# The first product of a gated layer in seven block products for eight, with its weights read from DRAM

## The chip, the cores and the metric

The kernel runs on one core of one Trainium2 chip. The metric is the device time of one launch in microseconds; host work on the arguments (reshaping and reordering) is not in it. A core has TensorE (PE) for matrix products, VectorE (DVE), ScalarE (ACT) and GpSimd (POOL) for elementwise work, and SyncE (SP), whose queue issues all of this kernel's DMAs. SBUF is the on-chip memory of 128 partitions, PSUM the accumulators: eight banks of 128x512 float32, all in use here.

## The reference

```python
x = attention(q, k, v, mem_k, mem_v)     # 4 batches, 8 heads, 768 tokens, 64 dims: chunks of 32
                                         # queries against 8 + 16 + 32 + 8 keys
x = x.transpose(0, 2, 1, 3).reshape(3072, 512)
gate = 1.0 / (1.0 + np.exp(-(x @ w_gate)))        # 512 x 1536
x = (gate * (x @ w_val)) @ w_out                  # 512 x 1536, 1536 x 512
h = x @ w_in                                      # 512 x 2048
g = h * (1.0 / (1.0 + np.exp(-h)))
out = g @ w_out2                                  # 2048 x 512
```

The five weights arrive as float64; q, k and v as float32.

## The kernel before

Every number that enters a large product is kept as two float32r parts, hi + lo (`split`: ScalarE copies hi, another engine subtracts it to get lo), and every product is three matmuls: hi·hi, hi·lo, lo·hi. One matmul has a 128x128 weight and 512 columns. The feature dimension of 512 is four tiles of 128 (`KT`), so `proj` issues 4 × 3 = 12 matmuls for a tile of 128 output features and 512 tokens, and `mm3` 12 for the four tiles of an output product.

The float64 weights are loaded raw (512 KB each of 128x512) and go through a pipeline of three steps (`Unit`, `Feed`): ScalarE scales the high words (L101), VectorE joins high and low words to a float32 in three instructions (`join`, L106, L109, L113), ScalarE and GpSimd split it (`part`).

*Layer 1* runs over six blocks of 512 tokens. Each has twelve f of 128 hidden features, and for each f TensorE does a gate product `pg`, a value product `pv` and, lagging one f, the output product into four banks `y` (L486 on): 36 matmuls. ScalarE takes the sigmoid, VectorE multiplies (`gated`, L264) and g is split. The attention of block b + 1 runs beside block b (`run_events`). The first block also prepares its own weights (`feed1`). `wo` is kept as plain float32 and split anew for each f of each block by ScalarE and GpSimd (`split_wo`). The finished block is copied out of PSUM (L429) and stored to DRAM (`yd`).

*Layer 2* runs over six blocks of 512 tokens with sixteen f each: twelve matmuls `ph` (L250), sigmoid (L260), multiplication (L264), split (L76, L79), and, lagging two f, twelve matmuls into the four banks `o` (`emit_out2`). All weights of layer 2 stay in SBUF; they are prepared by `feed2` in the last block of layer 1 and the first of layer 2, in slots that come free there. The x of the next block comes back from DRAM (`y32in`) and is split at the end of the block before.

The instructions stand in the order in which the code is written (`manual_schedule`); each engine runs its own queue in order, and a tile whose ring or pool is full waits for the last user of the old one.

Of the kernel before, what the change touches and what calls it, by code (L numbers as in the profile page):

```python
# [8 lines left out]
F32 = mybir.dt.float32  # L9
# [16 lines left out]
TPB = S // P  # attention tiles per batch row  # L26
# [4 lines left out]
BLOCKS2 = [512] * 6  # L31
# [7 lines left out]
NW = 2 * NF1  # resident gate and value units  # L39
# [3 lines left out]
def moe_kernel(ctx: ExitStack, tc: tile.TileContext, qh, kh, vh, wg, wv, wo, w2i, w2o, out):  # L43
# [14 lines left out]
    def w_slot(name):  # L58
        return main.tile([P, 2, 512], F32R, tag="w", name=name, bufs=NW)

    def t_slot(name):
        return main.tile([P, 512], F32, tag="t", name=name, bufs=2)
# [28 lines left out]
    class Unit:  # L91
        def __init__(self, src, name, raw_slot=None, slot=None):
            self.src, self.name, self.raw_slot, self.slot = src, name, raw_slot, slot

        def load(self):
            self.stg = main.tile([P, 512, 2], I32, tag="stg", name=f"stg_{self.name}", bufs=4)
            nc.sync.dma_start(out=self.stg.rearrange("p a b -> p (a b)"), in_=self.src)
# [5 lines left out]
        def join(self):  # L103
            self.t = (self.raw_slot or t_slot)(f"t_{self.name}")
# [9 lines left out]
                out=self.t.bitcast(I32), in0=high, scalar=3, in1=low,  # L114
# [3 lines left out]
        def part(self):  # L118
            if self.slot is not None:
                self.u = self.slot(self.name)  # L120
                split(self.u[:, 0], self.u[:, 1], self.t, nc.gpsimd)
# [113 lines left out]
    def split_x(src, n, name, on_pool=0, hi_dve=()):  # L235
        xs = []
        for kt in range(KT):
            x = main.tile([P, 2, 512], F32R, tag="x", name=f"{name}_{kt}", bufs=5)
# [6 lines left out]
    def proj(o, w, x, n, order=((0, 0), (0, 1), (1, 0)), late=None):  # L245
        """order: the products of parts (of w, of x) of each tile; late: the one kept for the end"""
# [23 lines left out]
    with tc.manual_schedule():  # L270
        att_cm = tc.tile_pool(name="att", bufs=1, side="right")
        att = att_cm.__enter__()
        wop_cm = tc.tile_pool(name="wop", bufs=1)
        wop = wop_cm.__enter__()

        NB1, NB2 = len(BLOCKS1), len(BLOCKS2)
        n0 = BLOCKS1[0] // P

        # buffers of the running attention, and those of the first tiles in weight slots
# [54 lines left out]
        # the first tiles, a step apart; idle products beforehand wake the tensor engine's clock  # L334
# [46 lines left out]
        # attention of block b + 1 runs beside the products of block b  # L381
# [26 lines left out]
        g_t, wo_u, yacc = {}, {}, {}  # L408

        def emit_out1(bi, f):  # L410
# [3 lines left out]
            g, w = g_t.pop((bi, f)), wo_u.pop((bi, f))  # L414
# [7 lines left out]
            mm3(groups)  # L422
            if f == NF1 - 1:
# [9 lines left out]
        def load_y(bi):  # L433
            t = x32_tile(f"y32in{bi}")
            lo, hi = sum(BLOCKS2[:bi]), sum(BLOCKS2[: bi + 1])
            for j, s in enumerate(starts1):
                a, b = max(lo, s), min(hi, s + BLOCKS1[j])
                if a < b:
                    nc.sync.dma_start(out=t[:, :, a - lo : b - lo], in_=y_dram[j][:, :, a - s : b - s])
            return t  # L440

        def split_wo(bi, f):
            w = wop.tile([P, 2, 512], F32R, tag="wor", name=f"wor{bi}_{f}", bufs=1)
# [191 lines left out]
```

## Time and profile before

| | before |
|---|---|
| median of three runs | 1255.85 us (1255.69 to 1255.92) |
| span of the profiled execution | 1254.8 us |
| TensorE busy, matmuls | 1213.5 us (97%), 6655 |
| VectorE, ScalarE, GpSimd busy | 564.1, 437.1, 206.5 us |
| moved by DMA | 93.30 MB, 74 GB/s over the span |
| last block of layer 1 begins, first `ph` of layer 2's fourth f | 602.20, 736.60 us |

The page's busy shares say which engine is full; the windows say in which stage. The chain of waits, followed back from the last instruction, is TensorE for most of its length. `PEclk` is the clock that TensorE was granted, 1.00 for 2.4 GHz.

### The profile page before, as it was taken

The numbers are of one execution on the slowest core, as the hardware profiler recorded it, in microseconds if no ns is written. First come the engines' busy times: TensorE is split into PE (matmuls) and PEld (weight loads), VectorE is DVE, ScalarE is ACT, GpSimd is POOL, SyncE is SP. The second block draws the span as 40 slices with busy tenths as digits, with TensorE's granted clock in tenths as the row PEclk, the third lists the DMA queues.
The fourth block names the chain that finished last, engine by engine and source line by source line (L and its number), as shares of the span: only waits on it lengthen the run. The fifth ranks groups of instructions, "written<-read, shape, count | busy, mean of one in ns | idle before, by whom it ended". The sixth has DMA issues, their size and how long they took to land.

```text
span 1254.8 us, 15980 instructions
## 1 busy us (share of the span) xinstructions
PE 1213.5 (97%) x6655; PEld 986.8 (79%) x6655; DVE 564.1 (45%) x780; ACT 437.1 (35%) x695; POOL 206.5 (16%) x156
## 2 busy tenths in 40 slices
PE   7888999999999999999978899999999999999999
PEld 6666788888888888888756688888888888888887
DVE  7999943333324333332688862332322322323322
ACT  3555543334334333333444442222322322222222
POOL 2555521111111111111345420000000000000000
PEclk9899999999999999999999999999999999999999
DMA  9666521213112121312454320000100100100000
GB/s 309 189 194 194 158 82 61 66 54 105 53 51 84 54 70 54 109 53 85 134 147 122 118 84 1 34 34 1 68 1 1 67 1 1 68 1 1 34 1 34
DMA packets 29016, 93.30 MB, mean 74 GB/s; under 512 B 3600, under 2 KB 3856, under 8 KB 28176
## 3 DMA queue, kind: packets, MB, share of 16 engines
q1 hardware_dynamic: 28944, 92.29, 23.5%
q8 instruction: 52, 0.85, 0.3%
q14 instruction: 20, 0.16, 0.0%
HBM read 79.69 MB, written 12.58 MB: 74 GB/s over the span
## 4 chain that ended last, share of the span: by engine, by line
PE 79%; DVE 17%; DMA 2%; issue 1%; ACT 1%; SPq 0%; DVEq 0%; ACTq 0%
PE ph L250 21%; PE pv L250 11%; PE pg L250 11%; PE o L88 7%; PE o L84 7%; PE o L86 7%; PE y L84 4%; PE y L86 4%; PE y L88 4%; PE sc L179 1%; DVE stg_w2i L109 1%; PE px L219 1%; DVE t_w2o L113 1%; DVE t_wg L113 1%; DVE t_wo L113 1%; DVE stg_w2i L106 1%
## 5 line engine op out<-in xcount | busy, mean ns | idle before, releaser
L250 PE MATMUL ph<-yy,w2i 128*128 128x512 f32 x1152 | 280.8, 393 | 2.5 <-ACT yy L76 1.4
L250 PEld LDWEIGHTS ph<-yy,w2i 128*128 128x128 f32 x1152 | 216.5, 189 | 49.6 <-ACT yy L76 1.8
L250 PE MATMUL pv<-x,wv 128*128 128x512 f32 x864 | 220.6, 406 | 24.4 <-DVE sg L264 22.9
L250 PEld LDWEIGHTS pv<-x,wv 128*128 128x128 f32 x864 | 164.5, 194 | 67.6 <-DVE sg L264 17.4
L250 PE MATMUL pg<-x,wg 128*128 128x512 f32 x864 | 210.4, 392 | 2.4 <-ACT wg L76 1.0
L264 DVE TENSOR_TENSOR sgh<-ph,sgh 128x512 f32<-128x512 f32 x96 | 66.4, 692 | 286.2 <-ACT sgh L260 286.1
L250 PEld LDWEIGHTS pg<-x,wg 128*128 128x128 f32 x864 | 160.6, 188 | 38.7 <-ACT wg L76 1.8
L79 POOL TENSOR_TENSOR wor<-t_wo,wor 128x512 fp32r<-128x512 f32 x72 | 100.4, 1395 | 394.1 <-ACT wor L76 394.1
L260 ACT ACTIVATE sgh<-ph 128x512 f32<-128x512 f32 x96 | 57.5, 599 | 296.6 <-PE ph L250 294.4
L88 PE MATMUL o<-w2o,gh 128*128 128x512 f32 (+1 forms) x384 | 148.1, 386 | 0.0
L86 PE MATMUL o<-w2o,gh 128*128 128x512 f32 (+1 forms) x384 | 148.0, 385 | 0.0
L84 PE MATMUL o<-w2o,gh 128*128 128x512 f32 (+1 forms) x384 | 147.9, 385 | 0.0
L264 DVE TENSOR_TENSOR sg<-pv,sg 128x512 f32<-128x512 f32 x72 | 49.3, 684 | 114.9 <-PE pv L250 114.8
L76 ACT CAST g<-sg 128x512 fp32r<-128x512 f32 x72 | 44.7, 621 | 151.0 <-DVE sg L264 151.0
L79 DVE TENSOR_TENSOR gh<-sgh,gh 128x512 fp32r<-128x512 f32 x96 | 66.5, 693 | 65.9 <-ACT gh L76 65.9
L76 ACT CAST gh<-sgh 128x512 fp32r<-128x512 f32 x96 | 59.5, 620 | 80.1 <-DVE sgh L264 80.1
L84 PEld LDWEIGHTS o<-w2o,gh 128*128 128x128 f32 x384 | 72.1, 188 | 15.3
L86 PEld LDWEIGHTS o<-w2o,gh 128*128 128x128 f32 x384 | 72.1, 188 | 15.3
L88 PEld LDWEIGHTS o<-w2o,gh 128*128 128x128 f32 x384 | 72.1, 188 | 14.7
L84 PE MATMUL y<-g,wor 128*128 128x512 f32 x288 | 79.5, 398 | 0.6 <-ACT wor L76 0.6
L86 PE MATMUL y<-g,wor 128*128 128x512 f32 x288 | 77.2, 390 | 0.0
L88 PE MATMUL y<-g,wor 128*128 128x512 f32 x288 | 77.0, 389 | 0.0
(85 smaller groups left out, 1123.1 us busy)
## 6 DMA issues: line engine op xcount, KB each, us to landing
k<-in_kh_dram SPq DMA_DIRECT2D x24, 512.0 KB, 5.2
qA<-in_qh_dram SPq DMA_DIRECT2D x21, 512.0 KB, 3.9
vA<-in_vh_dram SPq DMA_DIRECT2D x42, 256.0 KB, 4.2
stg_w2i<-in_w2i_dram SPq DMA_DIRECT2D x16, 512.0 KB, 3.6
stg_w2o<-in_w2o_dram SPq DMA_DIRECT2D x16, 512.0 KB, 3.6
stg_wg<-in_wg_dram SPq DMA_DIRECT2D x12, 512.0 KB, 4.0
stg_wv<-in_wv_dram SPq DMA_DIRECT2D x12, 512.0 KB, 3.6
stg_wo<-in_wo_dram SPq DMA_DIRECT2D x12, 512.0 KB, 3.7
```

Source lines behind the costliest of these rows:

```text
L76: nc.scalar.copy(hi, src)
L79: lo_eng.tensor_tensor(out=lo, in0=src, in1=hi.bitcast(F32), op=ALU.subtract)
L84: nc.tensor.matmul(o, w_hi, x_hi, start=first, stop=False)
L86: nc.tensor.matmul(o, w_hi, x_lo, start=False, stop=False)
L88: nc.tensor.matmul(o, w_lo, x_hi, start=False, stop=last)
L106: nc.vector.tensor_scalar(out=low, in0=low, scalar1=29, scalar2=None, op0=ALU.logical_shift_right)
L109: nc.vector.scalar_tensor_tensor(out=low, in0=high, scalar=-2147483648, in1=low, op0=ALU.bitwise_and, op1=ALU.bitwise_or,)
L113: nc.vector.scalar_tensor_tensor(out=self.t.bitcast(I32), in0=high, scalar=3, in1=low, op0=ALU.logical_shift_left, op1=ALU.bitwise_or,)
L179: nc.tensor.matmul(scv[cp * 64 : cp * 64 + 64, c2, a], qb[:, 4 * a + c].rearrange("p u q -> p (u q)"), kt[:, a, c], start=True, stop=True,)
L250: nc.tensor.matmul(o[:, :n], w[:, pw, kt * P : (kt + 1) * P], x[kt][:, px, :n], start=i == 0, stop=i == len(steps) - 1,)
L260: nc.scalar.activation(out=sg[:, :n], in_=psg[:, :n], func=AF.Sigmoid)
L264: nc.vector.tensor_tensor(out=sg[:, :n], in0=psv[:, :n], in1=sg[:, :n], op=ALU.mult)
```

## The change

Layer 2's first product works on three blocks of 1024 tokens, two halves of 512, and on pairs of f. With the feature dimension cut in two, the tokens in two and the pair of f in two, h is a 2 × 2 matrix of blocks, and seven products of six matmuls give it for eight (Strassen's scheme in Winograd's form). The seven operands of the weights are sums and differences formed once, in `prepare2`, split, and stored to DRAM (`w2i_d`); the seven operands of x (`x_parts`) are formed for each block. The products accumulate in three banks c1, c2, c3, which the adding engines read between two products of the same bank. GpSimd does one addition per pair. The output products of the pair before are the `fill` between the products; g of the first half is split at once, h's second half is kept in SBUF (`g2`), and its output products follow after the eight pairs.

`prepare2` runs one step at every second third of an f in layer 1's blocks 1 to 5; it replaces `feed2`. `wo` is split once, in the first block, stored (`wo_d`) and read back for every f of the later blocks (`load_wo`, three f ahead); `split_wo` is gone. In layer 2 the weights are read for every use: `load_w2i` a ring of five slots, `load_w2o` four slots, three f ahead.

```diff
-BLOCKS2 = [512] * 6
+NB2 = 3
+NPAIR = NF2 // 2
...
+        def prepare2():
...
+            for n, (k, f) in enumerate(seq):
+                u, p = u2[n], f // 2
+                u.rebias()
+                if k == "i":
...
+                    u.join(pair)
+                    if n + 3 < len(u2):
+                        u2[n + 3].load()
+                    yield
+                    if f % 2 == 0:
+                        continue
+                    for o, a, b, op in (
+                        (S1, A21, A22, ALU.add),
+                        (S3, A11, A21, ALU.subtract),
+                        (S2, S1, A11, ALU.subtract),
+                        (S4, A12, S2, ALU.subtract),
+                    ):
+                        nc.vector.tensor_tensor(out=f32s[:, o], in0=f32s[:, a], in1=f32s[:, b], op=op)
+                    yield
+                    for c in range(4):
+                        m = min(2, 7 - 2 * c)
+                        co = p1.tile([P, 2, 512], F32R, tag="co", name=f"co{p}_{c}")
+                        cv = co.rearrange("p a (m k) -> p a m k", m=2)[:, :, :m]
+                        split(cv[:, 0], cv[:, 1], f32s[:, 2 * c : 2 * c + m], nc.vector)
+                        nc.sync.dma_start(
+                            out=w2i_d[p, :, c // 2, :, 2 * (c % 2) : 2 * (c % 2) + m],
+                            in_=cv.bitcast(F32),
+                        )
+                        yield
+                else:
...
+                    co = p1.tile([P, 2, 512], F32R, tag="co", name=f"coo{f}")
+                    split(co[:, 0], co[:, 1], u.t, nc.vector)
+                    nc.sync.dma_start(out=w2o_d[f], in_=co.bitcast(F32))
+                    yield
...
+        def load_wo(k):
+            bi, f = k // NF1, k % NF1
+            if 0 < bi < NB1:
+                w = wo_slot(f"wor{bi}_{f}")
+                nc.sync.dma_start(out=w.bitcast(F32), in_=wo_d[f])
+                wo_u[bi, f] = w
...
+            xp[b] = []
+            part(0, b11)
+            yield
+            sub(t1, b12, b11)
+            sub(b11, b22, t1)
+            part(1, b11)
+            yield
+            part(2, t1)
...
+        def load_w2i(k):
+
+            if k < NB2 * NPAIR * 2:
+                p, h = k // 2 % NPAIR, k % 2
+                w = w_slot(7 + k % NRING, f"wq{k}")
...
+                nc.sync.dma_start(out=w[:, :, :m].bitcast(F32), in_=w2i_d[p, :, h, :, :m])
+                wq[k] = w
...
+        def pair2(b, p, bank, fill, tail):
...
+            load_w2i(k + 4)
+            c1, c2, c3 = bank(f"c1_{n}"), bank(f"c2_{n}"), bank(f"c3_{n}")
...
+            prod(c1, A11, True)
+            nc.scalar.copy(s1, c1)
+            if tail:
+                tail()
+            prod(c2, S2, True)
+            add(u2, c2, s1)
+            prod(c3, S1, True)
+            nc.scalar.copy(s5, c3)
+            nc.gpsimd.tensor_tensor(out=s5, in0=s5, in1=s1, op=ALU.add)
+            fill(0)
+            prod(c2, S3, False)
+            add(s5, c2, s5)
+            ga = g2_tile(fa, b)
+            gb = g2_tile(fb, b)
+            nc.scalar.activation(out=gb, in_=s5, func=AF.Sigmoid)
+            load_w2i(k + 5)
+            prod(c1, A12, False)
+            q11 = t2(f"q11_{n}")
+            nc.scalar.activation(out=q11, in_=c1, func=AF.Sigmoid)
+            mul(gb, s5, gb)
+            fill(1)
+            prod(c2, A22, False)
+            add(s1, c2, s1)
+            mul(q11, c1, q11)
+            q21 = t2(f"q21_{n}")
+            nc.scalar.activation(out=q21, in_=s1, func=AF.Sigmoid)
+            prod(c3, S4, False)
+            add(u2, c3, u2)
+            gs[b, 0, fa] = g_split(q11, f"g{n}a")
+            nc.scalar.activation(out=ga, in_=u2, func=AF.Sigmoid)
+            mul(q21, s1, q21)
+            gs[b, 0, fb] = g_split(q21, f"g{n}b")
+            g2[b, fa], g2[b, fb] = ga, gb
+            fill(2)
...
-                    if last and feed2.n - 2 < NPB + 2 * f:
-                        feed2.step()
+                    elif (it + i) % 2 == 0:
+                        next(prep, None)
+                    if last and (i == 2 and 1 < f < NF1):
+
+                        if f >= 3:
+                            next(xgen, None)
...
-                if pending is not None:
-                    split_wo(*pending)
...
+        p1_cm.__exit__(None, None, None)
+        p2_cm = tc.tile_pool(name="p2", bufs=1)
+        p2 = p2_cm.__enter__()
...
+            for f in range(NF2):
+                if f + 1 < NF2:
+                    gs[b, 1, f + 1] = g_split(g2[b, f + 1], f"gd{b}_{f + 1}")
+                for s in out2_steps(b, 1, f, o2):
+                    s()
+                if b + 1 < NB2 and f > 0:
+                    next(xgen, None)
```

TensorE in layer 2, before: the fifth f of the first block, then the output product of the third. `ph0_4` is the accumulator, `yy` the parts of x, `w2i4` the weight, `gh` the gated h.

```order
L250 MATMUL ph0_4_5896<-yy0_0_5700,w2i4_5134 128x512 x3
L250 MATMUL ph0_4_5896<-yy0_1_5703,w2i4_5134 128x512 x3
L250 MATMUL ph0_4_5896<-yy0_2_5706,w2i4_5134 128x512 x3
L250 MATMUL ph0_4_5896<-yy0_3_5709,w2i4_5134 128x512 x3
L84 MATMUL o0_0_5842<-w2o2_5057,gh0_2_5831 128x512
L86 MATMUL o0_0_5842<-w2o2_5057,gh0_2_5831 128x512
L88 MATMUL o0_0_5842<-w2o2_5057,gh0_2_5831 128x512
L84 MATMUL o0_1_5843<-w2o2_5057,gh0_2_5831 128x512
```

TensorE now, the third pair of the first block: `xp0_0` to `xp0_6` are the operands of x, `wq4` and `wq5` the two ring slots with the pair's weights, `g0_1a` and `g0_1b` g of the pair before.

```order
L668 MATMUL c1_0_2_6065<-xp0_0_5405,wq4_5854 128x512 x6
L668 MATMUL c2_0_2_6066<-xp0_1_5464,wq4_5854 128x512 x6
L668 MATMUL c3_0_2_6067<-xp0_2_5517,wq4_5854 128x512 x6
L88 MATMUL o0_0_0_5954<-w2or2_5852,g0_1a_6047 128x512
...
L92 MATMUL o0_0_2_5956<-w2or2_5852,g0_1a_6047 128x512
L668 MATMUL c2_0_2_6066<-xp0_3_5575,wq4_5854 128x512 x6
L668 MATMUL c1_0_2_6065<-xp0_4_5628,wq5_5918 128x512 x6
L88 MATMUL o0_0_3_5957<-w2or2_5852,g0_1a_6047 128x512
...
L92 MATMUL o0_0_1_5955<-w2or3_6022,g0_1b_6052 128x512
L668 MATMUL c2_0_2_6066<-xp0_5_5687,wq5_5918 128x512 x6
L668 MATMUL c3_0_2_6067<-xp0_6_5741,wq5_5918 128x512 x6
```

The runs of twelve `ph` became seven runs of six, on three accumulators that other engines read in between, and the output matmuls stand in three portions among them.

VectorE at the passage into layer 2, before: the last gate multiplication and split of layer 1, those of the first f of layer 2, two copies of layer 1's result, and the joins of the feed.

```order
L264 TENSOR_TENSOR sg5_11_5665<-pv5_11_5677,sg5_11_5665 128x512
L79 TENSOR_TENSOR g5_11_5713<-sg5_11_5665,g5_11_5713 128x512
L264 TENSOR_TENSOR sgh0_0_5746<-ph0_0_5730,sgh0_0_5746 128x512
L79 TENSOR_TENSOR gh0_0_5749<-sgh0_0_5746,gh0_0_5749 128x512
L429 COPY y32_5_1_5767<-y5_1_4991 128x512
L429 COPY y32_5_3_5773<-y5_3_4993 128x512
L106 TENSOR_SCALAR stg_w2i14_5608<-stg_w2i14_5608 128x512
L109 SCALAR_TENSOR_TENSOR stg_w2i14_5608<-stg_w2i14_5608 128x512
```

VectorE now at the same place:

```order
L273 TENSOR_TENSOR sg5_11_5805<-pv5_11_5807,sg5_11_5805 128x512
L83 TENSOR_TENSOR g5_11_5821<-sg5_11_5805,g5_11_5821 128x512
L650 TENSOR_TENSOR u2_0_0_5861<-c2_0_0_5857,s1_0_0_5859 128x512
L521 COPY y32_5_1_5899<-y5_1_5277 128x512
L521 COPY y32_5_3_5905<-y5_3_5279 128x512
L650 TENSOR_TENSOR s5_0_0_5860<-c2_0_0_5857,s5_0_0_5860 128x512
L653 TENSOR_TENSOR g2_0_1_5916<-s5_0_0_5860,g2_0_1_5916 128x512
L650 TENSOR_TENSOR s1_0_0_5859<-c2_0_0_5857,s1_0_0_5859 128x512
```

The joins are gone from here, and the two copies stand between the first two additions of the first pair.

SP's queue in layer 2, before: the last store of layer 1, the next x, the four stores of a block's output, the x after it.

```order
L430 DMA yd5_68<-y32_5_3_5773 128x512
L439 DMA y32in2_6283<-yd2_65 128x2048
L533 DMA out_0_dram<-ob0_0_6338 128x512
L533 DMA out_0_dram<-ob0_1_6344 128x512
L533 DMA out_0_dram<-ob0_2_6350 128x512
L533 DMA out_0_dram<-ob0_3_6356 128x512
L439 DMA y32in3_6809<-yd3_66 128x2048
```

SP now, in the third pair and the fourth:

```order
L578 DMA wq8_6063<-w2i_d_109 128x2048
L578 DMA wq9_6113<-w2i_d_109 128x2x768
L586 DMA w2or5_6127<-w2o_d_108 128x1024
L586 DMA w2or6_6166<-w2o_d_108 128x1024
L531 DMA ya1_6168<-yd2_65 128x2048
L533 DMA yb1_6170<-yd3_66 128x2048
L578 DMA wq10_6172<-w2i_d_109 128x2048
L578 DMA wq11_6222<-w2i_d_109 128x2x768
L586 DMA w2or7_6236<-w2o_d_108 128x1024
```

Four loads of weights per pair stand where there were none.

## Rows read from the trace of the kernel before

**Rows 1.** Page, part 1: busy us (share of the span) xinstructions of each engine.
```profile
PE 1213.5 (97%) x6655; PEld 986.8 (79%) x6655; DVE 564.1 (45%) x780; ACT 437.1 (35%) x695; POOL 206.5 (16%) x156
```

**Rows 2.** Windows, a layer-1 block, the last one, then layer 2: window, length, busy (xinstructions).
```profile
core 0: us, PE busy (x) PEld busy (x) DVE busy (x) ACT busy (x) POOL busy (x), PEclk, DMA share, GB/s
...
492.23:602.20 109.97, 109.97 (x705) 89.33 (x704) 37.18 (x60) 39.81 (x58) 16.05 (x12) 1.00 0.23 73
602.20:718.05 115.85, 102.71 (x433) 81.27 (x431) 97.76 (x108) 52.06 (x92) 54.35 (x38) 0.99 0.45 136
718.05:1254.80 536.75, 531.14 (x2364) 438.45 (x2364) 170.45 (x246) 144.67 (x243) 9.32 (x7) 1.00 0.07 26
```

**Rows 3.** Waits of PE, 600 to 735 us: total us, times, longest.
```profile
PE pv L250 <- DVE sg L264: 13.1, 10, 3.1
```

**Rows 4.** Chain, start of layer 2: start us, us, what.
```profile
721.06 4.37 PE ph L250 x11
...
728.17 5.61 PE ph L250 x24
...
736.60 2.76 PE ph L250 x12
```

**Rows 5.** Chain, the middle of layer 2.
```profile
802.05 2.72 PE ph L250 x12
807.49 2.81 PE ph L250 x12
...
835.24 2.72 PE ph L250 x12
```

**Rows 6.** Timeline, all engines, the end: start us, us, engine line op.
```profile
1251.79 0.37 ACT L530 COPY ob<-o_end 128x256 f32<-128x256 f32 x1 [0.90 <-PE o_end L88]
```

**Rows 7.** Timeline of DVE in the last layer-1 block, columns as before.
```profile
641.82 0.42 DVE L106 TENSOR_SCALAR stg_w2o<-stg_w2o 128x512 int32<-128x512 int32 x1
642.34 0.69 DVE L109 SCALAR_TENSOR_TENSOR stg_w2o<-stg_w2o 128x512 int32<-128x512 int32 x1
643.13 1.57 DVE L113 SCALAR_TENSOR_TENSOR t_w2o<-stg_w2o 128x512 int32<-128x512 int32 x1
644.62 0.68 DVE L264 TENSOR_TENSOR sg<-pv,sg 128x512 f32<-128x512 f32 x1
645.99 0.69 DVE L79 TENSOR_TENSOR g<-sg,g 128x512 fp32r<-128x512 f32 x1 [0.69 <-ACT g L76]
646.60 1.53 DVE L106 TENSOR_SCALAR stg_w2i<-stg_w2i 128x512 int32<-128x512 int32 x1
```

**Rows 8.** Page, part 5: group xcount | busy us, mean ns | idle before.
```profile
L264 DVE TENSOR_TENSOR sgh<-ph,sgh 128x512 f32<-128x512 f32 x96 | 66.4, 692 | 286.2 <-ACT sgh L260 286.1
...
L79 POOL TENSOR_TENSOR wor<-t_wo,wor 128x512 fp32r<-128x512 f32 x72 | 100.4, 1395 | 394.1 <-ACT wor L76 394.1
L260 ACT ACTIVATE sgh<-ph 128x512 f32<-128x512 f32 x96 | 57.5, 599 | 296.6 <-PE ph L250 294.4
```

**Rows 9.** Page, part 6: DMA issues, KB each, us to landing.
```profile
stg_w2i<-in_w2i_dram SPq DMA_DIRECT2D x16, 512.0 KB, 3.6
...
yd<-y SPq DMA_DIRECT2D x24, 256.0 KB, 2.8
```

**Rows 10.** Windows of the first layer-1 block and what precedes it.
```profile
0.00:31.40 31.40, 25.07 (x362) 20.90 (x362) 23.28 (x42) 10.45 (x17) 7.91 (x17) 1.00 0.96 308
31.40:62.70 31.30, 25.68 (x124) 19.65 (x123) 29.20 (x34) 17.06 (x26) 16.23 (x11) 0.89 0.63 189
62.70:94.10 31.40, 26.89 (x163) 20.64 (x162) 29.69 (x37) 17.52 (x28) 16.50 (x12) 0.95 0.65 194
94.10:125.50 31.40, 27.51 (x171) 21.48 (x170) 29.50 (x37) 15.71 (x25) 16.14 (x11) 0.98 0.63 195
125.50:156.90 31.40, 29.22 (x205) 22.69 (x204) 29.81 (x36) 16.28 (x27) 17.35 (x12) 0.97 0.54 158
```

**Rows 11.** Window of the first f of layer 2.
```profile
721.50:752.90 31.40, 31.40 (x131) 25.51 (x130) 21.80 (x31) 13.72 (x24) 7.78 (x6) 0.95 0.25 84
```

More of the change, by code (lines that the diff above doesn't have):

```diff
@@ L38 @@
 NP = 2
-NW = 2 * NF1
+NRING = 5
+A11, S2, S1, S3, A12, A22, S4, A21 = range(8)
 @with_exitstack
@@ L113, in join @@
             nc.vector.scalar_tensor_tensor(
-                out=self.t.bitcast(I32), in0=high, scalar=3, in1=low,
+                out=into.bitcast(I32), in0=high, scalar=3, in1=low,
                 op0=ALU.logical_shift_left, op1=ALU.bitwise_or,
@@ L118, in part @@
         def part(self):
-            if self.slot is not None:
-                self.u = self.slot(self.name)
-                split(self.u[:, 0], self.u[:, 1], self.t, nc.gpsimd)
+            self.u = self.slot(self.name)
+            split(self.u[:, 0], self.u[:, 1], self.t, nc.gpsimd)
+            if self.keep is not None:
+                nc.sync.dma_start(out=self.keep, in_=self.u.bitcast(F32))
     class Feed:
@@ L237, in split_x @@
         for kt in range(KT):
[L238 removed]
+            x = p1.tile([P, 2, 512], F32R, tag="x", name=f"{name}_{kt}", bufs=5)
             lo_eng = nc.gpsimd if kt >= KT - on_pool else nc.vector
@@ L404, in run_events @@
                     prefetch_v(t + 1)
-        g_t, wo_u, yacc = {}, {}, {}
+        def prepare2():
+            seq = []
+            for p in range(NPAIR):
+                seq += [("i", 2 * p), ("i", 2 * p + 1), ("o", 2 * p), ("o", 2 * p + 1)]
+            u2 = [
+                Unit((w2i if k == "i" else w2o)[f], f"w2{k}{f}") for k, f in seq
+            ]
+            for u in u2[:3]:
+                u.load()
+            f32s = None
+            for n, (k, f) in enumerate(seq):
[3 more added lines that the diff above has]
+                    if f % 2 == 0:
+                        f32s = p1.tile([P, 8, 256], F32, tag="f", name=f"f{p}")
+                        pair = f32s[:, A11 : A12 + 1 : A12 - A11]
+                    else:
+                        pair = f32s[:, A22 : A21 + 1 : A21 - A22]
+                    u.join(pair)
+                    if n + 3 < len(u2):
+                        u2[n + 3].load()
+                    yield
+                    if f % 2 == 0:
+                        continue
[17 more added lines that the diff above has]
+                        yield
+                else:
+                    u.join()
+                    if n + 3 < len(u2):
+                        u2[n + 3].load()
+                    yield
[3 more added lines that the diff above has]
+                    yield
@@ L431, in emit_out1 @@
                 del yacc[bi]
[L433 to L443, printed above, removed]
-            split(w[:, 0], w[:, 1], U1["o", f].t, nc.gpsimd)
-            wo_u[bi, f] = w
@@ new lines, in chunks, with out2_steps, step @@
+        def chunks(seq, n):
+            k = -(-len(seq) // n)
+            return [seq[i * k : (i + 1) * k] for i in range(n)]
+        def out2_steps(b, half, f, o):
+            k = (2 * b + half) * NF2 + f
+            steps = []
+            for i in range(4):
+                def step(i=i):
+                    g, w = gs[b, half, f], w2o_u[k]
+                    c = slice(i * P, (i + 1) * P)
+                    mm3([(o[i], g[:, 0, c], g[:, 1, c], w[:, 0], w[:, 1], f == 0, f == NF2 - 1)])
+                    if i == 3:
+                        load_w2o(k + 3)
+                steps.append(step)
+            return steps
@@ new lines, in out2_end @@
+        def out2_end(b, half, o):
+            t0 = b * 1024 + half * 512
+            for i in range(4):
+                ob = t2(f"ob{b}_{half}_{i}")
+                if b == NB2 - 1 and half == 1 and i == 3:
+                    for eng, d in ((nc.scalar.copy, slice(0, 256)), (nc.vector.tensor_copy, slice(256, 512))):
+                        eng(ob[:, d], o[i][:, d])
+                        nc.sync.dma_start(out=out[t0 + i * P : t0 + (i + 1) * P, d], in_=ob[:, d])
+                    continue
+                if i % 2 == 0:
+                    nc.scalar.copy(ob, o[i])
+                else:
+                    nc.vector.tensor_copy(ob, o[i])
+                nc.sync.dma_start(out=out[t0 + i * P : t0 + (i + 1) * P, :], in_=ob)
@@ L467, in moe_kernel, with g2_tile @@
+        g2 = {}
+        def g2_tile(f, b):
+            return p2.tile([P, 512], F32, tag=f"g2_{f}", name=f"g2_{b}_{f}")
+        pending = None
+        prep = prepare2()
+        xgen = None
         for bi, n in enumerate(BLOCKS1):
```

284 lines of the change are left out of this document (172 added, 112 removed).

## The prediction

> **What bounds the kernel now.** I read the page's busy shares first: TensorE is busy for 97% of the span [rows 1], so its instruction count sets the time wherever it runs without a gap. The windows by stage say where that holds. A middle block of layer 1 is busy for all of its 109.97 us, with VectorE at 37.18 and GpSimd at 16.05 [rows 2]; blocks 1 to 4 differ by 0.1 us. The last block of layer 1 takes 115.85 us, and there VectorE is busy for 97.76 of them [rows 2]. TensorE's waits between 600 and 735 us name the reason: ten value products (`pv`) waited 13.1 us for VectorE's gate multiplication [rows 3], which stood in its queue behind the joins of layer 2's weights. The chain gives the price of a matmul: one `ph` with the 12 output matmuls behind it takes 807.49 − 802.05 = 5.44 us, so 0.2267 us for each 128x512 matmul at a granted clock of 1.00 [rows 2, 5].
>
> Two sums show what the existing order loses. From 602.20 us, where the last block of layer 1 begins, to 736.60, where `ph` of f = 3 starts [rows 2, 4], TensorE issues 36 × 12 (layer 1, with the output product that lags one f) + 12 (its last output product) + 36 (`ph` 0 to 2) + 12 (the first `o`) = 492 matmuls, 111.52 us. The stretch is 134.40 us: 22.88 us are lost. From 736.60 to the end at 1254.80 there are 93 × 12 + 95 × 12 = 2256 matmuls, 511.36 us of 518.20: 6.84 us are not pitch. Of these, 3.1 lie behind the last matmul (ScalarE's last copy starts at 1251.79, the output DMA ends the span) [rows 6]; most of the rest is in the five f of each block that take 27.75 us for 27.20 (835.24 − 807.49, rows of 2.81) [rows 5], and in the halved tile of the last block.
>
> **The change, part by part.**
>
> *Fewer products.* Seven block products of six matmuls replace eight for every pair of f and 1024 tokens: 42 for 48. Three blocks of eight pairs: 24 × 6 = 144 matmuls fewer, layer 2 has 2160 for 2304. 144 × 0.2267 = 32.6 us.
>
> *Layer 1, blocks 1 to 4.* GpSimd's split of `wo` goes (12 a block; the block reads the split weights from DRAM, 512 KB per f of 8.16 us, requested three f ahead, against 3.6 us for such a load [rows 9]). Added are the joins, sums and splits that prepare layer 2, one step for every second third of an f. A join costs VectorE 0.42 + 0.69 + 0.69 = 1.80 us when GpSimd is idle, a split's low half 0.69 [rows 7, 8]. In all 32 joins (57.6), 32 sums of half a tile (bounded by 0.42 and 0.69; 0.5: 16) and 48 lows, 32 of them for the sums' weights (33): 107 us over five blocks, 21 each. VectorE goes from 37 to 58 of 110. A gate multiplication has an output product and a `pg`, 5.44 us, before the next `pv` needs its bank. The worst piece ahead of it is a join of 1.80, or a split that waits for the previous split's store (one buffer, 2.8 us for 256 KB, 3.6 for a load of 512 [rows 9]). I cost the edit at nothing; without this cover it is a stall like those of rows 3, up to 13.1 us a block.
>
> *The last block of layer 1.* The feed that made VectorE busy for 97.76 us is gone from here; 18 preparation steps and the seven parts of the first x (128x1024 each, twice a 128x512 row) remain: about 25 + 17 + gate work 24 × 0.69 = 17, some 58 of 97.9 us. GpSimd does nothing here. In the rows before, a 0.69 us join step takes 1.57 and a 0.42 one 1.53 where GpSimd's split of 1.4 us lies beside it, while a multiplication that reads PSUM stays at 0.68 [rows 7, 8]. I take 0.5 us of stall (between 0 and 13.1). By the Trainium skill, page "SBUF — State Buffer", section "Who interferes with whom", VectorE and GpSimd share one port pair as an exclusive lock, and a VectorE instruction with two SBUF inputs is blocked while GpSimd reads SBUF; by that rule the joins fall to their short form here, as the rows with idle GpSimd do, and GpSimd's new additions in layer 2 can block only the multiplications and splits there, not the additions that read PSUM.
>
> *Entry into layer 2.* The first tiles of the new pool lie where layer 1's lay, so ScalarE's copy of c1 waits for the last reader there, the last output product (fill 0). Behind it come the copy (0.60) and VectorE's u2 (0.69) before product S3 may write c2: with hand-overs TensorE waits about 1.8 us. Then VectorE's queue has the copy of the fourth y tile, which waits for the first y store (2.8 us) since they share a ring of three; s5 stands behind it, and product A22 waits for s5: 0.6 + 0.6 + 2.8 + 0.7 + 0.7 = 5.4, with some 1.0 us of hand-overs between five engines and queues, less the 4.5 us in which u2's wait and two products passed: 1.9 us taken. Together 3.7, between 1.3 (one copy and one addition) and 6.5 (the chain exposed whole). Before, the first matmuls after the pause ran slow: 11 took 4.37 for 2.49 us [rows 4], in a window of granted clock 0.95 [rows 11], so between 1.2 and 2.4 GHz. I keep 1.8 us for the same after the new pauses (0 to 2).
>
> *Steady pairs.* In a pair TensorE does 18 matmuls of products, 9 of fill, S3, A12, 9 of fill, A22, S4 and 6 of fill: 66, or 14.96 us. VectorE has ten instructions of 0.69 in it, ScalarE eight of 0.60, GpSimd one near 1.4 [rows 8]. The tightest hand-over: s5 needs c3's copy and GpSimd's addition, 2.0 us, under fill 0's 2.04; then S3 (1.36), the addition (0.69), and A22 comes 3.40 us after S3 ends: slack above 2 us. The first pairs of blocks 1 and 2 have no fill; there I count 0.6 us each, 1.2.
>
> *Weights from DRAM.* 1.75 MiB of `w2i` products per pair and 0.5 MiB of `w2o` per f and half: 42 + 48 MiB, with y and out 102 MiB = 107 MB in some 498 us, 215 GB/s. In the first 31.4 us the DMA engines moved 308 GB/s at a share of 0.96; at 189 to 195 their share was 0.63 to 0.65 [rows 10], which puts the stream at about 0.7. Ring and lookahead (two pairs' halves, three f of 2.72 us against 3.6 us) cover it: nothing. All operands are now in main pools, and the slow five f (with the halved tile, 3.6 us in all) go.
>
> **Sum.** To 602.20 unchanged. Then 432 + 12 + 2160 = 2604 matmuls: 590.2. Stalls: 0.5 + 3.7 + 1.8 + 1.2 = 7.2. Tail 3.1. Span 1202.7. The median of the runs stands 1.05 above the profiled span (1255.85 to 1254.8), so 1203.8. As a difference: −32.6 (matmuls) − 22.9 + 6.0 (the passage into layer 2) − 3.6 + 1.2 (slow f against block heads) = −51.9.
>
> **Rivals.**
>
> *The pairs stall (late VectorE or ScalarE).* Ten VectorE instructions in a fixed order, each waiting for something, with a single-tile product behind: a lag of 0.5 to 1.0 us in each of 24 pairs, or the last block's 13.1 us unmended, gives 1216 to 1228. For it: today's own waits are such queueing [rows 3]; against: two microseconds of slack.
>
> *The clock falls between short groups.* If the handovers pause TensorE as often as the first block's did, where the granted clock was 0.89 to 0.98, mean 0.95 [rows 10], 2160 matmuls cost 489.6 × (1/0.9475 − 1) = 27 us more: 1231. Against: layer 2 has none of VectorE's 29 us in 31.4 that made the pauses there [rows 10]. The Trainium skill, "TensorE: Matmul & The Clock Gate", section "A second HAM failure mode: psum-queue depth-cycling", warns of just this cycling through accumulator banks; the existing layer 2 cycles through two banks at 1.00 [rows 2].
>
> *Preparation stalls blocks 1 to 4.* If 21 us more of VectorE cost each block what the last one pays now, 13.1 us [rows 3], 4 × 13.1 = 52 returns it to 1256: no change. Against: 58 of 110 us busy, not 98 of 116.
>
> *The stream bounds layer 2 (slower).* If 192 GB/s, the rate of the first block's windows [rows 10], is what such loads reach with stores and compute beside them, 107 MB take 557 us for the 498 planned: 1203.8 + 59 = 1263. It decides from 107 / (498 + 52) = 195 GB/s down. Against: the 308 of the first window, and a first block whose rate its demand explains.
>
> **Chances.** Forecast 0.77 (its own range 1196 to 1211); pairs or last block 0.12; clock 0.04; preparation 0.02; stream 0.05. A measurement of this kernel tells 0.2%, 2.5 us, from no change. Slower is the stream, 0.05; same 0.02; faster the rest, 0.93. For the range: what falls below 1195 (0.03) and above 1220 (half the pair case, the clock, preparation and stream, 0.17) is left out.
>
> **What would show it.** Layer 1's blocks 1 to 4 at 109.97 us with VectorE near 58; block 5 near 98 us, with hardly a row of `pv` waiting for VectorE; two waits of about 1.8 us in the first pair, the second behind VectorE's y copy; then pairs of 14.96 us, a clock of 1.00, GB/s near 215 at a share near 0.7. The forecast is wrong if pairs take 15.5 us or more, if the waits of `c` name VectorE or a DMA in most pairs, or if the windows of blocks 1 to 4 grow.

## The result, and the profile after

The changed kernel takes 1202.56 us (median of four runs, 1201.16 to 1203.49) for 1255.88 of the kernel before beside it: ratio 0.9575, 95% interval 0.9562 to 0.9589. The prediction was 1203.8 with a range of 1195 to 1220. The profiled execution has a span of 1201.2 us; the median lies 1.4 above it.

Page of the changed kernel, part 1, answering to [rows 1]:

```profile
PE 1170.9 (97%) x6463; PEld 953.8 (79%) x6463; DVE 637.0 (53%) x965; ACT 441.4 (37%) x696; POOL 110.8 (9%) x88
```

Windows of the changed kernel: layer 1's blocks 2, 3 and 6, layer 2, then two pairs (columns as in [rows 2]):

```profile
162.21:273.39 111.18, 110.80 (x706) 89.02 (x704) 56.13 (x100) 41.73 (x63) 1.30 (x1) 1.00 0.67 223
273.39:383.36 109.97, 109.97 (x705) 89.33 (x704) 56.35 (x99) 40.76 (x62) 0.00 (x0) 1.00 0.60 200
...
603.31:701.23 97.92, 97.92 (x434) 81.08 (x433) 48.59 (x69) 30.31 (x48) 0.00 (x0) 1.00 0.52 181
701.23:1201.20 499.97, 493.69 (x2173) 407.16 (x2171) 223.19 (x324) 164.37 (x269) 30.92 (x24) 1.00 0.60 205
```
```profile
761.35:776.31 14.96, 14.96 (x68) 12.39 (x67) 6.57 (x11) 4.82 (x9) 1.29 (x1) 1.00 0.55 194
776.31:791.27 14.96, 14.96 (x68) 12.39 (x67) 6.57 (x11) 4.81 (x9) 1.29 (x1) 1.00 0.55 193
```

Layer 1's last block, 115.85 us in [rows 2], is now 97.92, its 432 matmuls at 0.2267 us and not one gap. A pair takes 14.96 us, its 66 matmuls exactly, at a granted clock of 1.00, with VectorE busy for 6.57 of them. The stream moves 205 GB/s at a share of 0.60.

| stretch | predicted | measured |
|---|---|---|
| to layer 1's last block | 602.20 | 603.31 |
| last block | 98.4 | 97.92 |
| 2172 matmuls from there | 492.3 | 492.3 |
| entry into layer 2 (waits, slow clock) | 5.5 | 3.0 |
| first pairs of the other two blocks | 1.2 | 0.7 |
| behind the last matmul | 3.1 | 3.9 |
| span | 1202.7 | 1201.2 |

The measured rest is from the starts of layer 2's three blocks, 701.23, 870.15 and 1033.73: 168.92 us for 732 matmuls (165.92), 163.58 for 720 (163.20), and 167.47 to the end.

The entry, in TensorE's timeline of the changed kernel, answering to [rows 4]:

```profile
701.23 4.24 PE L668 MATMUL c<-xp,wq 128*128 128x512 f32 x18
...
709.59 3.01 PE L668 MATMUL c<-xp,wq 128*128 128x512 f32 x12 [1.40 <-DVE u L650]
713.61 7.09 PE L668 MATMUL c<-xp,wq 128*128 128x512 f32 x30 [1.01 <-DVE s L650]
```

The two forecast waits stand where they were forecast. The 30 matmuls behind the second take 7.09 us; a row of 30 with no stop before it shows 6.96 (they follow each other by 0.2267 us, and the last one is 0.39 long). The clock did not fall as it had in [rows 4, 11].

### The profile page after: what moved, and what is told of

It reads as the page before. It is cut to its first block, busy times and chain, and to the rows that moved or that the text cites. A ratio compares the mean times of both kernels' runs of the same rounds, so it can differ in the third digit from the quotient of the medians.

```text
span 1201.2 us, 16298 instructions
## 1 busy us (share of the span) xinstructions
PE 1170.9 (97%) x6463; PEld 953.8 (79%) x6463; DVE 637.0 (53%) x965; ACT 441.4 (37%) x696; POOL 110.8 (9%) x88
## 4 chain that ended last, share of the span: by engine, by line
PE 78%; DVE 12%; issue 4%; DMA 4%; ACT 1%; SPq 0%; POOL 0%; DVEq 0%; POOLq 0%; ACTq 0%
PE c L668 17%; PE pv L259 13%; PE pg L259 13%; PE o L92 6%; PE o L90 6%; PE o L88 6%; PE y L88 5%; PE y L90 4%; PE y L92 4%; PE sc L187 1%; PE px L227 1%; DVE t_wg L120 1%; DVE t_wo L120 1%; DVE t_wv L120 1%; DVE stg_wv L116 1%
## 5 line engine op out<-in xcount | busy, mean ns | idle before, releaser
L668 PE MATMUL c<-xp,wq 128*128 128x512 f32 x1008 | 239.9, 390 | 2.5 <-DVE u L650 1.4
L259 PE MATMUL pv<-x,w 128*128 128x512 f32 x864 | 216.4, 400 | 13.0 <-DVE sg L273 11.5
L668 PEld LDWEIGHTS c<-xp,wq 128*128 128x128 f32 x1008 | 188.9, 188 | 43.3 <-DVE s L650 2.4
L259 PE MATMUL pg<-x,w 128*128 128x512 f32 x864 | 210.6, 392 | 1.5 <-POOL x L83 0.9
L259 PEld LDWEIGHTS pv<-x,w 128*128 128x128 f32 x864 | 163.0, 192 | 52.3 <-issue 14.5
L259 PEld LDWEIGHTS pg<-x,w 128*128 128x128 f32 x864 | 160.4, 188 | 38.1 <-ACT x L80 1.4
L269 ACT ACTIVATE sg<-pg 128x512 f32<-128x512 f32 x72 | 42.9, 596 | 142.5 <-PE pg L259 130.4
L88 PE MATMUL o<-w2or,gd 128*128 128x512 f32 x192 | 74.7, 389 | 0.0
L90 PE MATMUL o<-w2or,gd 128*128 128x512 f32 x192 | 74.7, 389 | 0.0
L92 PE MATMUL o<-w2or,gd 128*128 128x512 f32 x192 | 74.7, 389 | 0.0
L83 DVE TENSOR_TENSOR g<-sg,g 128x512 fp32r<-128x512 f32 x60 | 41.5, 692 | 43.4 <-ACT g L80 43.4
L90 PEld LDWEIGHTS y<-g,wor 128*128 128x128 f32 x240 | 45.1, 188 | 9.6
L92 PEld LDWEIGHTS y<-g,wor 128*128 128x128 f32 x240 | 45.0, 188 | 9.4
L88 PEld LDWEIGHTS y<-g,wor 128*128 128x128 f32 x240 | 43.8, 188 | 9.6 <-issue 0.8
```

Source lines behind the costliest of these rows:

```text
L88: nc.tensor.matmul(o, w_hi, x_hi, start=first, stop=False)
L90: nc.tensor.matmul(o, w_hi, x_lo, start=False, stop=False)
L92: nc.tensor.matmul(o, w_lo, x_hi, start=False, stop=last)
L259: nc.tensor.matmul(o[:, :n], w[:, pw, kt * P : (kt + 1) * P], x[kt][:, px, :n], start=i == 0, stop=i == len(steps) - 1,)
L269: nc.scalar.activation(out=sg[:, :n], in_=psg[:, :n], func=AF.Sigmoid)
L668: nc.tensor.matmul(o, w[:, pw, i % 4, kt * P : (kt + 1) * P], X[i][:, px, kt], start=first and j == 0, stop=j == 5, skip_group_check=not f ...
```

## The experiments

Each run is compared with the 1202.56 us of the changed kernel, unless another is named; the kernel before ran beside each at 1255.8 to 1256.5.

**One product more, one less.**

```diff
             prod(c3, S4, False)
+            prod(c3, S4, False)
```

> Does the seventh product twice in every pair (h is wrong by it): eight block products, as many matmuls in the first product as the kernel before, all else as changed. If the saved product is worth its matmuls and nothing else, the time rises by 144 x 0.2267 = 32.6 us to 1235, and the remaining 21 us to the kernel before belong to the other parts (last block of layer 1, entry, slow f). Rival, the pairs had hidden waits that the product covers: a rise under 25.

1235.21 us: 32.65 more (two runs, 1233.76 and 1236.65). In the trace a pair takes 16.32 us for 14.96, and layer 2 takes 532.65 for 499.97. The saved product is worth its 144 matmuls.

```diff
-            prod(c3, S4, False)
```

> Leaves the seventh product (S4) out of every pair, so part of h is wrong; 24 x 6 = 144 matmuls fewer. If only TensorE's instruction count sets the time of the pairs (slack of 2 us at the hand-overs, a weight stream below what the DMA engines give), a pair takes 60 x 0.2267 = 13.60 us and the time falls by 32.6 us to about 1170. Rival, the hand-overs or the stream are nearly the bound already: the pairs stay above 14.2 us, and the time above 1184.

1173.22 us: 29.3 less, of which 28.1 in layer 2 (471.84 us for 499.97). Its pairs take 13.60 us, so 32.6 is gained there; TensorE now waits three times for the split of the last pair's g (2.0 us in all, 3.6 with the stops around them). The next limit of a pair lies below 13.60 us; nothing here finds it.

**Density or the shared port.**

```diff
-                        split(cv[:, 0], cv[:, 1], f32s[:, 2 * c : 2 * c + m], nc.vector)
+                        split(cv[:, 0], cv[:, 1], f32s[:, 2 * c : 2 * c + m], nc.gpsimd)
...
-                    split(co[:, 0], co[:, 1], u.t, nc.vector)
+                    split(co[:, 0], co[:, 1], u.t, nc.gpsimd)
```

> The low halves of layer 2's prepared weights (48 instructions in layer 1's blocks 1 to 5) go back from VectorE to GpSimd, where the kernel before had them. Theory, the last block's stalls came from the density of the joins (27 units in one block), the port between VectorE and GpSimd only added to it: join steps beside a GpSimd split show 1.5 us again, VectorE's busy time in a block changes by less than 10 us, and the time stays within 3 us. Rival, GpSimd beside the joins is the cause by itself: value products wait for VectorE again, 5 us or more a block, 20 us or more in all.

1201.60 us, ratio to the kernel before 0.9566 (0.9552 to 0.9580): no difference. VectorE and GpSimd in this run's last block of layer 1, from the timelines:

```profile
617.48 1.33 DVE L83 TENSOR_TENSOR g<-sg,g 128x512 fp32r<-128x512 f32 x1 [0.69 <-ACT g L80]
...
625.63 1.53 DVE L113 TENSOR_SCALAR stg_w2i<-stg_w2i 128x512 int32<-128x512 int32 x1
```
```profile
616.98 1.29 POOL L83 TENSOR_TENSOR coo<-t_w2o,coo 128x512 fp32r<-128x512 f32 x1 [10.67 <-ACT coo L80]
625.59 1.29 POOL L83 TENSOR_TENSOR coo<-t_w2o,coo 128x512 fp32r<-128x512 f32 x1 [7.33 <-ACT coo L80]
```

A join step of 0.42 us takes 1.53 and a split of 0.69 takes 1.33, as in [rows 7]: each ends as if its work had begun about where GpSimd's instruction ends (618.27 and 626.88). That costs nothing here, with nine such GpSimd instructions in the block (38 in the kernel before) and VectorE busy for 47 us of 97.92.

```diff
...
                         next(prep, None)
+                    if last:
+                        for _ in range(2):
+                            nc.vector.tensor_tensor(out=scr, in0=scr, in1=scr, op=ALU.add)
```

> Two idle VectorE additions of 0.69 us (on a scratch tile) after every third of an f in the last block of layer 1: 36 x 2 x 0.69 = 49.7 us more, so VectorE would be busy for 98 of the block's 97.9 us, as densely as before the change (97.76 of 115.85), with GpSimd idle. If density is what made the value products wait, they wait again: 10 us or more in this block, time 1212 or more. Rival, it needs GpSimd's splits on the shared port beside it: the block stays within 3 us of 97.9.

1215.23 us. Window of the last block and TensorE's waits from there to the first pairs of layer 2, in this run:

```profile
601.40:712.05 110.65, 102.29 (x433) 81.16 (x432) 92.53 (x139) 28.78 (x47) 0.00 (x0) 0.98 0.43 152
```
```profile
PE pv L259 <- DVE sg L273: 5.6, 5, 2.9
PE pg L259 <- ACT sg L269: 2.8, 2, 2.5
```

The block takes 12.7 us more, with GpSimd idle, and the wait of [rows 3] is back at the head of the list: 5.6 us for 13.1. TensorE is idle for 8.4 us and busy for 4.4 more, at a granted clock of 0.98; in [rows 2] it was 13.1 and 4.8. Density alone makes 12.7 of the 17.9 us that the block lost before the change.

**The entry.**

```diff
-                    y32 = main.tile([P, 512], F32, tag="sg", name=f"y32_{bi}_{dm}", bufs=3)
+                    if dm < 3:
+                        y32 = main.tile([P, 512], F32, tag="sg", name=f"y32_{bi}_{dm}", bufs=3)
+                    elif bi < NB1 - 1:
+                        y32 = t_slot(f"y32_{bi}_{dm}")
+                    else:
+                        y32 = t2(f"y32_{bi}_{dm}")
...
-            return p2.tile([P, 512], F32, tag="t2", name=name, bufs=8)
+            return p2.tile([P, 512], F32, tag="t2", name=name, bufs=7)
...
+                        ob = t2(f"ob{b}_{half}_{i}e")
...
+            if b == 0 and p == 0:
+                s1, s5, u2 = (xr.tile([P, 512], F32, tag="t3", name=f"{a}_{n}", bufs=3) for a in ("s1", "s5", "u2"))
...
```

> The two waits at the entry into layer 2 taken away: s1, s5 and u2 of the very first pair lie in a free place instead of layer 1's old one, and the fourth y tile has a tile outside the ring of three, in every block. The two halves of the last output tile also get a tile each. By the trace of the changed kernel that is worth 1.4 + 1.0 us at the entry, 1.2 in the second block of layer 1, where the fourth y copy holds up the joins and the gate behind it, and 0.4 at the end: 4 us, so about 1198.5. Rival, the next hand-over takes the place of each (GpSimd's addition in the first pair, the join in the second block): 2 us or less.

1197.65 us (five runs, 1196.99 to 1197.89), ratio 0.9528 (0.9515 to 0.9541): the fastest kernel of this study, its interval below that of the changed kernel. TensorE's timeline at the entry, and the windows of layer 1's second block and of layer 2:

```profile
698.89 4.24 PE L674 MATMUL c<-xp,wq 128*128 128x512 f32 x18
...
705.69 9.68 PE L674 MATMUL c<-xp,wq 128*128 128x512 f32 x42
```
```profile
161.01:271.05 110.04, 110.04 (x706) 89.26 (x704) 56.08 (x100) 41.69 (x63) 1.29 (x1) 1.00 0.66 224
698.89:1195.80 496.91, 493.07 (x2173) 407.40 (x2171) 223.35 (x324) 165.62 (x269) 30.90 (x24) 1.00 0.60 207
```

No wait is left at the entry. By the windows the edit is worth 1.1 us in the second block and 3.1 in layer 2. The other 1.2 us between the two spans lie before 162 us, where the edit has no instruction; that stretch came out between 160.7 and 163.4 in the profiles of the changed kernel and its variants. The end gained nothing:

```profile
1192.10 0.37 ACT L643 COPY ob<-o 128x256 f32<-128x256 f32 x1
...
1192.51 0.42 DVE L643 COPY ob_3e<-o 128x256 f32<-128x256 f32 x1 [1.07 <-DMA out_dram<-ob]
```

VectorE's copy still begins only where ScalarE's ends. Both read one PSUM bank, but the row names a store; what holds it is not shown.

**Slack in a pair.**

```diff
             prod(c2, S3, False)
+            for _ in range(5):
+                add(scr, c2, scr)
             add(s5, c2, s5)
...
```

> Five VectorE additions of 0.69 us that read c2 (into a scratch tile) between product S3 and the addition s5 in every pair: 3.45 us on the tightest hand-over. In the changed kernel's trace s5 is done 2.44 us before product A22 begins. If that is the slack, A22 comes 1.0 us late in each of 24 pairs: 24 us, 1227. Rival, VectorE's later work in the pair is pushed on too and the pairs lose the whole 3.45: 83 us, 1285. Rival, the slack is larger than the trace shows: no change.

1240.21 us: 37.6 more. Steady pairs in TensorE's timeline of this run:

```profile
765.51 3.02 PE L668 MATMUL c<-xp,wq 128*128 128x512 f32 x12 [0.88 <-DVE s L650]
...
781.65 3.02 PE L668 MATMUL c<-xp,wq 128*128 128x512 f32 x12 [0.88 <-DVE s L650]
```

16.14 us a pair, 1.18 more. The additions put s5 off by 3.51 us, 1.07 beyond the slack of 2.44. TensorE loses the 0.88 that the row shows, 0.16 in which the last matmul before it runs out (its row is 0.39 us long at a pitch of 0.2267), and 0.14 in the twelve behind (3.02 for 2.88). So the slack is as read, and a stop costs 0.3 us beyond the wait in its row. 21 such pairs make 25 us. The rest falls where there is no fill: 4.5 us of wait in the first pair of the first block, 2.9 in those of the other two; and behind the 4.5 the clock is low, which the chain of this run and the window show:

```profile
716.36 9.15 PE c L668 x30
```
```profile
716.36:726.00 9.64, 9.64 (x33) 7.80 (x34) 5.77 (x9) 4.50 (x8) 0.00 (x0) 0.77 0.37 127
```

30 matmuls in 9.15 us, for 7.09 after the changed kernel's wait of 1.0. Behind the two waits of 2.92 us, in the second and the third block, the clock stayed once and fell once:

```profile
893.11 7.10 PE L668 MATMUL c<-xp,wq 128*128 128x512 f32 x30 [2.92 <-DVE s L650]
...
1067.83 8.74 PE L668 MATMUL c<-xp,wq 128*128 128x512 f32 x30 [2.92 <-DVE s L650]
```
```profile
893.11:901.70 8.59, 8.59 (x38) 7.12 (x39) 5.79 (x9) 4.60 (x8) 0.79 (x1) 1.00 0.38 128
1067.83:1076.50 8.67, 8.67 (x31) 6.97 (x32) 5.37 (x9) 4.01 (x7) 0.00 (x0) 0.80 0.34 115
```

**What hides the stream.**

```diff
-                        load_w2o(k + 3)
+                        load_w2o(k + 2)
...
-        for k in range(3):
+        for k in range(2):
             load_w2o(k)
```

> The output weights of layer 2 are requested two f ahead instead of three, so in the second halves one f (2.72 us) before they are needed. If the lookahead is what hides the stream, a load that lands in 4.7 us leaves TensorE 2.0 us late in each of 48 f: 95 us, 1298. Rival, such a load lands as fast as the shortest of before (3.6 us) when little else is under way: 0.9 x 48 = 43 us, 1246. If loads are hidden anyway: no change.

1202.58 us: no change; both numbers expected were wrong. SyncE's queue in a second half, in the changed kernel and then in this run:

```profile
832.26 27.52 SPq L586 DMA_DIRECT2D w2or<-w2o_d  x11
```
```profile
832.11 27.55 SPq L586 DMA_DIRECT2D w2or<-w2o_d  x11
```

The loads go out at the same times in both, one for each f of 2.72 us. A request's place in the order of the code is not when it starts; SyncE runs ahead, and the load starts when its slot is free.

```diff
-            return main.tile([P, 2, 512], F32R, tag="wo", name=name, bufs=4)
+            return main.tile([P, 2, 512], F32R, tag="wo", name=name, bufs=2)
...
-            load_wo(bi * NF1 + f + 3)
+            load_wo(bi * NF1 + f + 1)
...
-                        load_w2o(k + 3)
+                        load_w2o(k + 1)
...
-        for k in range(3):
+        for k in range(1):
```

> The run with requests two f ahead instead of three changed nothing, so where the request stands in the order may not be what hides the loads; SyncE runs ahead and a load starts when its slot is free. Here the ring of output weights has two slots instead of four (requests one f ahead in the order). If the number of slots is the cover, a load starts one f (2.72 us) before its use in the second halves and lands after 3.6 to 4.7: TensorE waits 0.9 to 2.0 us in each of 48 f, 43 to 95 us, 1246 to 1298. Rival, the loads are hidden even so: no change.

1346.57 us: 144 more, above both ends. TensorE's waits, one of them in its timeline, the windows around it, in a first half, and that of layer 2:

```profile
PE o L88 <- DMA w2or<-w2o_d: 91.9, 40, 4.1
```
```profile
790.01 0.50 PE L88 MATMUL o<-w2or,g_3b 128*128 128x512 f32 x1 [3.65 <-DMA w2or<-w2o_d]
```
```profile
775.00:787.00 12.00, 11.36 (x51) 9.07 (x49) 5.70 (x9) 4.74 (x8) 1.29 (x1) 1.00 0.37 120
787.00:796.00 9.00, 5.99 (x19) 4.78 (x20) 1.29 (x2) 0.55 (x2) 0.00 (x0) 0.81 0.40 160
796.00:803.00 7.00, 7.00 (x33) 5.79 (x32) 3.87 (x6) 3.03 (x6) 0.79 (x1) 1.00 0.45 152
...
700.00:1341.80 641.80, 539.30 (x2171) 426.08 (x2169) 223.22 (x324) 164.61 (x269) 30.95 (x24) 0.94 0.47 161
```

The waits for loads make 92 us, near the upper end, but that is luck: 74 of them, 22 stops of up to 4.1 us, lie in the first halves, where I had expected none, and the second halves have 17.6 us in 18 stops, where I had expected 43 or more. In the first halves the second load of a pair starts only when the first slot of the fill comes free (read from the order, not tested). Behind such a wait the granted clock shows 0.81 in the window, between its two levels of 1.2 and 2.4 GHz; over layer 2 it is 0.94. Against the changed kernel TensorE is idle for 96 us more in layer 2 and busy for 46 more, for the most part by the lower clock (estimated: 0.06 of 539 us is 32). Layer 1, whose loads use the same two slots, lost nothing (between 162.2 and 700 us TensorE is busy throughout). Two slots are too few, four are enough. Three were not tried, nor four with requests one f ahead.

```diff
+                z = xr.tile([P, 640], F32, tag="z", name=f"z{k}", bufs=2)
+                nc.sync.dma_start(out=z, in_=w2o_d[k % NF2].rearrange("p a b -> p (a b)")[:, :640])
```

> A load of 320 KB more for every f and half of layer 2 (96 of them, into tiles that nobody reads): 31.5 MB on top of 107, 277 GB/s for 205. If the stream has the room that the share of 0.6 says, TensorE does not notice: 1202 within 3 us. Rival, the stream is close to what loads reach beside stores (the third rival of the prediction, at another rate): layer 2 grows by 10 us or more, with waits of c or o for a DMA.

1201.93 us: no change. Layer 2 of this run:

```profile
701.00:1199.00 498.00, 492.42 (x2168) 406.14 (x2166) 223.08 (x324) 164.37 (x269) 30.95 (x24) 1.00 0.74 268
```

268 GB/s at a share of 0.74 leave TensorE without a wait. The 192 GB/s of [rows 10] were demand, not a ceiling.

**The slow f.** The kernel before, with a tile of 32 bytes above the five right-hand weight tiles, which by the layout moves them to multiples of 64 bytes (the traces hold no addresses):

```diff
+                    if i == 0:
+                        pad = wb[0].tile([P, 8], F32, tag="pad", name="pad")
+                        nc.gpsimd.memset(pad, 0.0)
...
```

> The kernel before with its five right-hand weight tiles of layer 2 moved by 32 bytes, so that they begin at multiples of 64 bytes as all other matmul operands do; nothing else. If the start address makes the slow f (2.81 and 2.76 us for 2.72), all f of layer 2 take 5.44 us, a block 87.04 for 87.59, and the time falls by about 3 us, to 1253. Rival, they are slow because of the end of the memory they lie in, or of what runs beside them: no change.

1255.60 us, ratio to the kernel before 0.9994 (0.9984 to 1.0003). From its chain, against [rows 5]:

```profile
806.69 2.80 PE ph L250 x12
812.24 2.80 PE ph L250 x12
817.79 2.80 PE ph L250 x12
```

The f are as slow as before, so the address's remainder is not the cause. The other way round, in the changed kernel:

```diff
-            return p2.tile([P, 2, 512], F32R, tag="gp", name=name, bufs=4)
+            g_turn[0] += 1
+            return (gr if g_turn[0] % 2 else p2).tile([P, 2, 512], F32R, tag="gp", name=name, bufs=2)
...
+                gr_cm = tc.tile_pool(name="gr", bufs=1, side="right")
...
```

> Half of layer 2's g tiles (TensorE's weights in the output products, those of even f in the first halves) lie at the upper end of SBUF, where the kernel before had its five slow weight tiles; the order of all engines is the same. If the place makes matmuls slow, every second output product takes 2.81 us for 2.72, and layer 2 about 4 us longer. Rival, what ran beside those f made them slow: no change, all at 2.72.

One run, 1208.14 us, span 1206.4 for 1201.2; layer 2 takes 505.61 us for 499.97. A pair in TensorE's timeline; `g_2a` lies at the upper end, `g_2b` does not:

```profile
746.22 4.24 PE L671 MATMUL c<-xp,wq 128*128 128x512 f32 x18
750.30 0.39 PE L88 MATMUL o<-w2or,g_2a 128*128 128x512 f32 x1
...
752.40 2.92 PE L671 MATMUL c<-xp,wq 128*128 128x512 f32 x12
755.16 0.39 PE L88 MATMUL o<-w2or,g_2a 128*128 128x512 f32 x1
...
757.24 2.88 PE L671 MATMUL c<-xp,wq 128*128 128x512 f32 x12
...
761.32 4.24 PE L671 MATMUL c<-xp,wq 128*128 128x512 f32 x18
```

15.10 us a pair for 14.96, with no new wait. The 18 matmuls before `g_2a` take 4.08 us, their pitch; the nine with `g_2a` take 2.10 for 2.04, the twelve behind them 2.76 for 2.72, the three with `g_2a` and six with `g_2b` 2.08 for 2.04, and from 757.24 on all is at pitch again. So the loss begins with the operand at the upper end, both times, and is spread in the rows over some matmuls behind it as well. The place makes matmuls slow; why, and how far down it reaches, was not tried.

## Why the prediction was right

*The matmuls.* The price of 0.2267 us from one `ph` and its outputs held for products of six: pairs of 14.96 us, and 32.65 us for the product put back.

*The last block.* Forecast at 0.5 us of stall, measured none; 17.9 us came from it (115.85 to 97.92). VectorE was busy for 48.59 us of it, where I had added up 58. I had weighed the port beside the density. The dense run makes 12.7 us of it with GpSimd idle, and the run with GpSimd's splits makes none, so density is shown as sufficient and the port alone, at nine GpSimd instructions in the block, as harmless here. What the port added before, where both came together, was not separated. On the rule in the Trainium skill, "SBUF — State Buffer", "Who interferes with whom", the trace agrees: VectorE's split with two SBUF inputs takes 1.33 us beside GpSimd's and 0.69 without.

*The preparation at nothing.* Right in blocks 3 to 5 of layer 1 (109.97 or 109.98 us), wrong in the second block: 111.18. The step that failed is the worst piece ahead of a gate multiplication, which I took to be one join, or one split that waits for a store. VectorE, then TensorE, in the changed kernel there:

```profile
177.22 0.69 DVE L521 COPY y<-y 128x512 f32<-128x512 f32 x1 [2.53 <-DMA yd<-y]
177.83 0.42 DVE L113 TENSOR_SCALAR stg_w2i<-stg_w2i 128x512 int32<-128x512 int32 x1
...
182.48 0.68 DVE L273 TENSOR_TENSOR sg<-pv,sg 128x512 f32<-128x512 f32 x1
```
```profile
183.22 3.06 PE L259 MATMUL pv<-x,w 128*128 128x512 f32 x12 [0.20 <-DVE sg L273]
186.46 0.63 PE L217 MATMUL pt<-ident,e 128*128 128x128 f32 x4 [0.18 <-DVE e L211]
```

The fourth y copy waits for a store; a join, attention and four sums stand behind it, then the multiplication, late for the next `pv`. The kernel before had nearly the same wait of the copy (2.27 us) with less behind it, and TensorE did not wait in that block at all. I had seen that copy at the entry and not here. The entry run gives it back.

*The entry.* Both waits stood where and behind what I had worked out, but shorter: 1.4 and 1.0 us for 1.8 and 1.9 (with the hand-over 1.56 and 1.30 between the starts less 30 and 12 matmuls). The second was too large because the store landed in 2.4 us and the hand-overs I added were shorter. The 1.8 us for a low clock failed: it stayed at 1.00 behind waits of 1.0 to 1.4, and fell behind 4.5 (the run with five additions) and 3.7 (two slots); behind 2.92 it did either. I had taken the term over from the entry before the change, where two waits stood close together ahead of the slow matmuls of [rows 4]:

```profile
719.41 0.51 PE L250 MATMUL ph<-yy,w2i 128*128 128x512 f32 x1 [1.36 <-ACT yy L76]
721.06 4.37 PE L250 MATMUL ph<-yy,w2i 128*128 128x512 f32 x11 [1.15 <-DVE yy L79]
```

There one matmul lies between the two waits; in the changed kernel twelve do.

The fall that the Trainium skill describes for cycling through accumulator banks ("TensorE: Matmul & The Clock Gate", "A second HAM failure mode: psum-queue depth-cycling"), by short idle times between the groups, did not come here: three banks in groups of six, idle only in the three first pairs, at 1.00 for all of layer 2.

*The slow f* went, worth what the rows said, but not for a reason I had shown; the place in SBUF is it.

*The stream.* Its price, nothing, was right; of the cover I named, ring and lookahead, requests two f ahead instead of three changed nothing, and two slots instead of four cost 144 us. It is the number of slots.

*The end* cost 0.8 us that I did not see. In the changed kernel's timeline, answering to [rows 6]:

```profile
1197.48 0.37 ACT L638 COPY ob<-o 128x256 f32<-128x256 f32 x1
...
1197.88 0.42 DVE L638 COPY ob<-o 128x256 f32<-128x256 f32 x1 [1.07 <-ACT ob L638]
```

The halves of the last tile now share a bank, and their copies come one after the other; that the bank is the reason was not tested.

The misses are 1.1 + 0.8 us against 0.5 + 2.5 + 0.5 and leave 1.6 us, so part of the closeness is luck. Of the rivals, the clock, stalled pairs and the stream did not come, and the preparation came only as the 1.1 us. Each can be made: the clock and the stream by two slots, the pairs by more than 2.4 us on s5.

## What to carry to other kernels

Where TensorE is busy for all of a stage, a term worked out as matmuls times pitch held to a tenth of a microsecond here (97.92 us for 432, 14.96 for 66); look for the misses at the seams, where a pool, a ring or a bank changes hands. Read an engine's load by the stage: VectorE busy for half of a block took 20 us more for nothing; at 84% (92.53 of 110.65) it stopped TensorE. What hid the loads that SyncE issues was their number of slots, not where the request stood.

## What the runs showed of the hardware

- With every second g tile in the uppermost 8 KB of a partition's SBUF (by the layout), a pair of 66 matmuls, 12 of them with such a weight, took 0.14 us more. In the kernel before, with five weight tiles in the uppermost 20 KB, 12 matmuls took 2.81 us for 2.72. A move by 32 bytes to multiples of 64 made no difference (1255.60 us).
- A stop of TensorE costs more than the wait in its row: 1.18 us a pair for 0.88.
- The granted clock stayed at 1.00 behind single waits of 1.4 us, stayed once and fell once (0.80 in the window) behind 2.92, and showed 0.81 in the window behind 3.65.
